# The order of the last loads on SyncE's queue, and a pool of their own for the last modulation products

## The chip, the cores and the metric

The kernel runs on one core of one Trainium2 chip. The metric is the time of one execution on the device in microseconds (us), of which the kernel before has three runs; beside them stands one execution recorded by the hardware profiler. The engines are named as in the profile: PE (TensorE matmuls; PEld is its weight load), DVE (VectorE), ACT (ScalarE), POOL (GpSimd) and SP (SyncE). SP computes nothing here: its queue (SPq) issues nearly all DMA transfers, one after the other.

## The reference

The kernel computes the output and all gradients of one adaLN-conditioned block. With x of shape 1x2048x512 (S = 2048 rows, D = 512 columns), F = 1792, and six modulation rows of 512 from `silu(c) @ w_mod`:

```python
mod = (_silu(c) @ w_mod).reshape(c.shape[0], 6, 1, -1)
sa, ca, ga, sb, cb, gb = (...)
h = _layernorm(x) * (1 + ca) + sa
x = x + ga * irfft2(rfft2(h) * (A_w_r + 1j * A_w_i))
h = _layernorm(x) * (1 + cb) + sb
r = relu(h @ w1 + b1)
x = x + gb * ((r * r) @ w2 + b2)
_out, _vjp = jax.vjp(_f, A_x, A_w_r, A_w_i, B_w1, B_b1, B_w2, B_b2, c, w_mod)
_grads = _vjp(grad_out)
```

Ten arrays come out: the block's output, and the gradients of x, of the two spectral filters, of w1, b1, w2, b2, c and w_mod. All are bfloat16.

## The kernel before

The 2048 rows lie as 16 row tiles of 128 rows (`NT = 16`), handled in pairs t = 0, 2, ..., 14. The 1792 hidden columns are 14 blocks of 128 (`NFC = 14`), numbered 0 to 13 here. The Fourier transforms are matmuls with tables of sines. The kernel goes forward through the spectral part and the two-layer part, then back; the forward part and most of the backward one end about 325 us into the span. What follows, and what the change touches, is the last stage (lines 1399 to 1513), in which four kinds of work are interleaved:

- **The gradient of w2**, `grad_w2` (line 1378). For each hidden block, PE adds up 16 matmuls (L1386) with the transposed block `hns[fc]` as weights and the scaled output gradient `g_sb` as the moving side. ACT copies the sum to a `gw` tile (L1387), and SPq stores it (L1388). Blocks 10 and 13 are done in two halves of 256 columns. The order of the products is 0, 1, 3, 2, 4, 5, 6, 7, 8, 9, first half of 10, 11, 12, second half of 10, both halves of 13.
- **The loads of the blocks**, `load_hn` (line 1201). Block fc was written to `h_dram` earlier, and comes back as a transposing DMA of 512 KB (L1206). Blocks 4 to 13 go into a ring of six tiles, `hn` 0 to 5, in the pool `endp`: block 4 is tile hn_0s, block 9 is hn_5s, and blocks 10, 11, 12, 13 take over tiles hn_0s, hn_1s, hn_2s, hn_3s, so that each must wait until PE is done with block 4, 5, 6 or 7.
- **The last step of the gradient of x**, for each pair of row tiles: `row_pair` (line 1448) and `row_end` (line 1470). PE makes the inverse transform (L372, L382), ACT copies it out (L1456), and DVE and ACT go back through the first normalisation. This reads two tiles per pair that `load_rows3` (line 1275) brings in: the normalised rows `n1` (L1279; shown as n, n_0s or n_1s in the profile) and the gradient so far, `gxl` (L1280). They go round between three places: the pairs t = 4 and 10 use n and gxl, t = 0, 6 and 12 use n_0s and gxl_0s, and t = 2, 8 and 14 use n_1s and gxl_1s. So the load for t = 14 must wait until DVE and ACT have done with the rows of t = 8. With `q1 = gh1 * n1` (L1461) PE adds up column sums into `acc1` (L1443).
- **The last two products of the modulation gradient**, `gm.emit` (line 454) for j = 0 and 1. After the last column sums ACT copies half of `acc1` (L1494) and DVE adds the halves to `acc1_sb` (L1496). A matmul (L459) spreads the row over 128 partitions, ACT copies it to `gmbc` and scales it into `gwm` (L468), and DVE multiplies it with a quarter of a slice of w_mod each time (L471; its `gm_junk` result is thrown away, only the sum is kept). `gm.load` (line 449) brings the slices, `wmc`, in.

The last lines add up the gradient of c: DVE (L1506, L1508), a transposing matmul (L1510), a copy (L1512) and a store (L1513, tile gcr).

**Pools.** A `Slots` pool gets one stretch of each partition's memory and a tile per name and buffer number; when a pool is released, a later one may take its memory over. The first instruction of an engine that uses such a new pool then waits for all that still uses the old memory. Line 1431 makes the pool `endp` when the last product of the w1 gradient is done. In the kernel before it holds the ring of blocks, the `gw`, `gh1`, `q1` and `gs` tiles, and the tiles of the last two modulation products as well.

**The order of the instructions** is written out by hand: `ORDER` (line 477) has a string of numbers per engine. Each number is an instruction of that engine in the order in which the program's text makes them, and `set_order` (line 574) chains the instructions in the order of the string. No planner chooses anything. An engine's queue is in order, SPq's too: if one instruction there waits for a semaphore, all behind it wait. DMA transfers share eight completion semaphores in turn, so a transfer also waits for the landing of the eighth before it.

Of the kernel before, what the change touches and what calls it, by code (L numbers as in the profile page):

```python
# [11 lines left out]
FP32 = mybir.dt.float32  # L12
BF16 = mybir.dt.bfloat16
# [5 lines left out]
D = 512  # L19
# [250 lines left out]
def unfold(nc, pool, y, w, n, name):  # L270

    u = pool.tile([P, n, 2, 2, P], BF16, name=name, bufs=1)
    w2 = w.rearrange("p n (e c d) -> p n e c d", e=2, c=2)
    nc.vector.tensor_tensor(u[:, :, 0], w2[:, :, 0], w2[:, :, 1], op=ALU.add)
    nc.vector.tensor_tensor(u[:, :, 1], w2[:, :, 0], w2[:, :, 1], op=ALU.subtract)
    y4 = y.rearrange("p n (k d) -> p n k d", k=4)
    nc.vector.tensor_tensor(y4[:, :, 0:4:2, :], u[:, :, :, 0], u[:, :, :, 1], op=ALU.add)
    nc.vector.tensor_tensor(y4[:, :, 3:0:-2, ::-1], u[:, :, :, 0], u[:, :, :, 1], op=ALU.subtract)
# [88 lines left out]
def spec_g2(tc, K, CS, t, tpool, pool, ahead=0):  # L367

    nc = tc.nc
    ps = pool.tile([P, D], FP32, name="psT")  # L370
    for i in range(4):
        nc.tensor.matmul(ps[:, P * i:P * i + P], lhsT=CS[:, t, i].rearrange("p a b -> p (a b)"), rhs=K["Cf"][:, i, :], start=True, stop=True)  # L372
    Tsb = tpool.tile([P, D], BF16, name="Tsb", bufs=4 if ahead else 2)
    K["Tsb"] = nc.scalar.activation(Tsb, ps, AF.Copy, scale=EF_S).ins
    return Tsb


def spec_g3(tc, K, Tsb, pool):

    nc = tc.nc  # L380
    psY = pool.tile([P, D], FP32, name="psY")
    nc.tensor.matmul(psY, lhsT=K["TAT"], rhs=Tsb, start=True, stop=True)  # L382
    return psY
# [57 lines left out]
class GMod:  # L441
# [12 lines left out]
    def emit(self, jc, q, row, pool, ppool, nbuf=2, last=False):  # L454
# [110 lines left out]
        "137 143 149 158 146 150 112 132 164 83 145 144 165 161 166 160 162 168 159 163 169 171 154 167 170 173 172 175 147 174 "  # L565
        "178 186 176 188 209 185 190 193 177 191 210 183 195 204 223 192 187 194 189 207-208 180 215 200 197 196 202 206 217 205 "
        "216 211 181 179 199 203 213 225 218 201 220 198 219 212 182 184 214 224 222 221 229 236 227 237 228 226 233 232 231 230 "
        "241 234 247 235 246 253 267-268 239 251-252 260 245 243 255 240 242 272 244 249 274 264 256 258 257 269 262 276 259 250 "
        "254 263 271 275 238 261 279 277-278 270 265-266 248 283 282 284 280 285 287 281 286 288 273 289"
    ),  # L570
}
# [22 lines left out]
def kernel(  # L594
# [602 lines left out]
    gm = GMod(tc, K, scf, gsc, wm_view, out9_view)  # L1197
    hnp = Slots(tc, name="hnp", bufs=1, side="right")
    hns, endp = [], {}
# [67 lines left out]
    def run_later(n=1):  # L1267
        if later:
            later[0][0] -= n
            if later[0][0] <= 0:  # L1270
                later.pop(0)[1]()
# [3 lines left out]
    def load_rows3(t):  # L1275
        if t < NT:
            pool, n = (endp["fp"], 1) if t % 6 == 4 else (fin, 2)
            rows3[t] = [pool.tile([P, 2, D], BF16, name=x, bufs=n) for x in ("n1", "gxl")]
            nc.sync.dma_start(rows3[t][0], n1_dram[t // 2])  # L1279
            K["rows"] = nc.sync.dma_start(rows3[t][1], gx1_dram[t // 2]).ins  # L1280
# [22 lines left out]
    def fill_w1(n):  # L1303
        for _ in range(n):
            if units:
                units.pop(0)()
# [110 lines left out]
    psX = Slots(tc, name="psX", bufs=1, space=PSUM)  # L1417
# [6 lines left out]
    def fill(n):  # L1424
        for _ in range(n):
            if units:
                fill_w1(1)
                if not units:
                    gwa.release()
                    gap.release()  # L1430
                    endp["hn"] = endp["gm"] = Slots(tc, name="endp", bufs=2)
            elif units2:
                units2.pop(0)()
                run_later()

    with Slots(tc, name="psE", bufs=2, space=PSUM) as psE, Slots(tc, name="psS1", bufs=1, space=PSUM) as psS1:

        acc1 = psS1.tile([P, D], FP32, name="acc1")
        late = Delayed(2)

        def colsums1(t, gh1, q1):
            for q, row in ((0, gh1[:, 0, :]), (32, q1[:, 0, :]), (64, gh1[:, 1, :]), (96, q1[:, 1, :])):
                nc.tensor.matmul(acc1[q:q + 32, :], lhsT=K["ones_q"], rhs=row, start=(t == 0), stop=(t == NT - 2), tile_position=(0, q))  # L1443

        def g2_pair(t):
            return [spec_g2(tc, K, CS, t + i, fp, psE, 60) for i in range(2)] if t < NT else None

        def row_pair(t, Ts):
            n1, gxl = rows3[t]
            gh1, q1 = [(endp["gm"].tile([P, 2, D], BF16, name=x, bufs=3) if "gm" in endp and t >= 6 else fp.tile([P, 2, D], BF16, name=x, bufs=2)) for x in ("gh1", "q1")]  # L1450
            gn = fp.tile([P, 2, D], BF16, name="gn")
            gs = (endp["gm"].tile([P, 2, D], BF16, name="gs", bufs=6) if "gm" in endp and t >= 6 else fp.tile([P, 2, D], BF16, name="gs", bufs=3))
            rr = fp.tile([P, 2, 4], FP32, name="rr")
            for i in range(2):
                psY = spec_g3(tc, K, Ts[i], psE)
                nc.scalar.copy(out=gs[:, i, :], in_=psY)  # L1456
            unfold(nc, fp, gh1, gs, 2, "unf_u")
            nc.vector.tensor_tensor(gn, gh1, modb[:, CA1_B, None, :].broadcast_to([P, 2, D]), op=ALU.mult)
            for i in range(2):
                nc.scalar.activation(gs[:, i, :], gn[:, i, :], AF.Copy, scale=inv1[:, t + i:t + i + 1], accum_out=rr[:, i, 0:1])  # L1460
            nc.vector.tensor_tensor(q1, gh1, n1, op=ALU.mult)  # L1461
            late.add(lambda: colsums1(t, gh1, q1))
            for i in range(2):
                jk = fp.tile([P, D], BF16, name="jk1", bufs=1)
                nc.vector.scalar_tensor_tensor(out=jk, in0=gs[:, i, :], scalar=K["onef"], in1=n1[:, i, :], op0=ALU.mult, op1=ALU.mult,
                                               accum_out=rr[:, i, 1:2])
            nc.vector.tensor_scalar(rr[:, :, 2:4], rr[:, :, 0:2], -1.0 / D, None, op0=ALU.mult)
            return t, n1, gxl, gn, gs, rr

        def row_end(t, n1, gxl, gn, gs, rr):  # L1470
            for i in range(2):
                nc.scalar.activation(gn[:, i, :], n1[:, i, :], AF.Identity, scale=rr[:, i, 3:4], bias=rr[:, i, 2:3])
            nc.vector.tensor_tensor(gs, gn, gs, op=ALU.add)
            gx = gs
            nc.vector.tensor_tensor(gx, gs, gxl, op=ALU.add)
            nc.sync.dma_start(out1_view[:, t:t + 2, :], gx)
            load_rows3(t + 6)

        Ts = g2_pair(0)
        for t in range(0, NT, 2):  # L1480
            fill(1)
            pair = row_pair(t, Ts)
            Ts = g2_pair(t + 2)
            if t < NT - 2:
                row_end(*pair)
            fill(1 if t % 4 == 0 and t < 12 else 0)
            if t == 10:
                grad_b2()
                gm.load(0, endp["gm"])
                gm.load(1, endp["gm"])  # L1490
        fill(3)
        late.flush()
        acc1_odd = endp["gm"].tile([64, D], FP32, name="acc1_odd", bufs=1)
        K["Tsb"] = nc.scalar.copy(out=acc1_odd, in_=acc1[64:128, :]).ins  # L1494
        acc1_sb = endp["gm"].tile([64, D], BF16, name="acc1_sb", bufs=1)
        nc.vector.tensor_tensor(acc1_sb, acc1[0:64, :], acc1_odd, op=ALU.add)  # L1496
        row_end(*pair)
        fill(1)
        for j in range(2):
            gm.emit(j, 32 * j, acc1_sb[32 * j:32 * j + 1, :], endp["gm"], psX, 4, True)  # L1500
            fill(1)
        while units2:
            fill(1)

        gst = fp.tile([P, 4], FP32, name="gst")
        nc.vector.tensor_reduce(gst, gsc.rearrange("p j d -> p d j"), axis=mybir.AxisListType.X, op=ALU.add)  # L1506
        gcb = fp.tile([P, 4], BF16, name="gcb")
        nc.vector.scalar_tensor_tensor(out=gcb, in0=t1, scalar=-1.0, in1=gst, op0=ALU.mult, op1=ALU.mult)  # L1508
        pg = psX.tile([4, P], BF16, name="mm")
        nc.tensor.transpose(pg, gcb, K["ident"])  # L1510
        gcr = fp.tile([4, P], BF16, name="gcr", bufs=1)
        nc.vector.tensor_copy(gcr, pg)  # L1512
        nc.sync.dma_start(out_8.rearrange("b (dc p) -> (b dc) p", p=P), gcr)  # L1513
# [8 lines left out]
    cdp.release()  # L1522
    cfp.release()
    utcs.release()
    endp["gm"].release()
    set_order(tc)

# [32 lines left out]
```

## Time and profile before

| | |
|---|---|
| median of 3 runs | 406.19 us (405.02 to 406.92) |
| the profiled execution | 405.56 us |
| its span, first to last instruction | 403.8 us |
| granted TensorE clock, mean | 0.991 |
| PE busy | 385.1 us (95%) |
| DVE busy | 341.9 us (85%) |
| ACT busy | 278.3 us (69%) |
| packets of the busiest DMA queue, share of 16 engines' span | 90.0% |

Busy time is the union of an engine's instructions; a pipelined matmul counts until its modelled end. The waits name, for each idle spot of an engine, the line that ran after it and what ended it. A row of a timeline gives start and duration in us, the engine, the line, and what is written from what. A DMA row of SPq is the issue alone, from the moment when its waits are over until the queue is free again; the transfer lands later. The trace's semaphore updates give the time of each landing (the completion marks).

### The profile page before, as it was taken

The numbers are of one execution on the slowest core, as the hardware profiler recorded it, in microseconds if no ns is written. First come the engines' busy times: TensorE is split into PE (matmuls) and PEld (weight loads), VectorE is DVE, ScalarE is ACT, GpSimd is POOL, SyncE is SP. The second block draws the span as 40 slices with busy tenths as digits, with TensorE's granted clock in tenths as the row PEclk, the third lists the DMA queues.
The fourth block names the chain that finished last, engine by engine and source line by source line (L and its number), as shares of the span: only waits on it lengthen the run. The fifth ranks groups of instructions, "written<-read, shape, count | busy, mean of one in ns | idle before, by whom it ended". The sixth has DMA issues, their size and how long they took to land.

```text
span 403.8 us, 6936 instructions
## 1 busy us (share of the span) xinstructions
PE 385.1 (95%) x2403; PEld 201.8 (50%) x2428; DVE 341.9 (85%) x831; ACT 278.3 (69%) x501; POOL 14.0 (3%) x56
## 2 busy tenths in 40 slices
PE   4899999999999999999999999899999999899887
PEld 1345566765444444444444444455655665444345
DVE  5989978969896899989898999938789967697795
ACT  4569899889870695279536857358667546898595
POOL 4520100000000000000000000000000000000000
PEclk9699999999999999999999999999999999999999
DMA  8999999587595899779977889969999999999997
GB/s 251 239 210 280 238 205 273 157 193 262 160 217 111 215 217 199 178 171 235 206 208 160 201 206 237 272 187 302 279 274 271 256 326 161 192 259 236 232 270 262
DMA packets 141643, 90.97 MB, mean 225 GB/s; under 512 B 95778, under 2 KB 127528, under 8 KB 141096
## 3 DMA queue, kind: packets, MB, share of 16 engines
q1 hardware_dynamic: 140900, 89.93, 90.0%
q10 hardware_dynamic: 708, 0.59, 0.5%
q8 instruction: 19, 0.31, 0.3%
q14 instruction: 16, 0.13, 0.1%
HBM read 36.35 MB, written 33.19 MB: 172 GB/s over the span
## 4 chain that ended last, share of the span: by engine, by line
PE 64%; DVE 12%; ACT 8%; SPq 7%; DMA 6%; issue 2%; DVEq 0%; ACTq 0%
PE og_0s L1042 8%; PE og_1s L1042 8%; PE mm_0s L1287 6%; PE mm_1s L1287 5%; PE mm_1s L1386 4%; PE mm_1s L841 4%; PE mm_1s L1013 4%; PE mm_0s L1386 3%; PE mm_0s L841 3%; PE mm_0s L1013 3%; DMA w2T<-in_B_w_dram 3%; PE pst L1013 2%; SPq L1206 2%; SPq L693 2%; ACT AE L336 2%
## 5 line engine op out<-in xcount | busy, mean ns | idle before, releaser
L1287 PEld LDWEIGHTS <-h_sb 128*128 128x128 bf16 x256 | 24.7, 98 | 21.4 <-issue 0.4
L1042 PEld LDWEIGHTS <-gab 128*128 128x128 bf16 x224 | 21.5, 98 | 25.1 <-DVE gab L1020 0.6
L1013 PEld LDWEIGHTS <-w 128*128 128x128 bf16 x224 | 21.3, 98 | 25.0 <-issue 1.7
L841 PEld LDWEIGHTS <-w2T 128*128 128x128 bf16 x224 | 21.2, 98 | 22.3 <-issue 2.9
L1287 PE MATMUL mm_0s<-gab,h_sb 128*128 128x384 bf16 (+1 forms) x160 | 30.2, 342 | 0.0
L1042 PE MATMUL og_0s<-w1T,gab 128*128 128x512 bf16 x110 | 25.7, 379 | 0.4 <-DVE gab L1020 0.3
L1042 PE MATMUL og_1s<-w1T,gab 128*128 128x512 bf16 x108 | 25.3, 379 | 0.2
L336 ACT ACTIVATE AE<-psB 128x1024 bf16<-128x1024 f32 x16 | 22.2, 1387 | 2.6 <-PE psB L332 2.6
L1013 PE MATMUL mm_1s<-h2T,w 128*128 128x512 bf16 x84 | 21.6, 379 | 0.0
L1287 PE MATMUL mm_1s<-gab,h_sb 128*128 128x512 bf16 (+1 forms) x96 | 20.8, 370 | 0.0
L1013 PE MATMUL mm_0s<-h2T,w 128*128 128x512 bf16 x80 | 20.5, 379 | 0.0
L841 PE MATMUL mm_1s<-gT_0s,w2T 128*128 128x512 bf16 x56 | 15.4, 394 | 0.9 <-DMA w2T<-in_B_w_dram 0.8
L841 PE MATMUL mm_0s<-gT_0s,w2T 128*128 128x512 bf16 x56 | 15.3, 397 | 0.8 <-DMA w2T<-in_B_w_dram 0.5
L372 PEld LDWEIGHTS <-utcs 128*128 128x128 bf16 x128 | 10.3, 97 | 10.4 <-issue 4.1
L1013 PE MATMUL pst<-h2T,w 128*128 128x512 bf16 x60 | 15.4, 379 | 0.0
L841 PE MATMUL mm_1s<-gT_1s,w2T 128*128 128x512 bf16 x56 | 14.4, 379 | 0.1
L841 PE MATMUL mm_0s<-gT_1s,w2T 128*128 128x512 bf16 x56 | 14.4, 379 | 0.1
L1386 PE MATMUL mm_0s<-g_sb,hn_1s 128*128 128x512 bf16 x62 | 14.2, 379 | 0.1
L845 ACT CAST gab<-mm_1s 128x512 bf16<-128x512 f32 x20 | 12.4, 621 | 2.3 <-PE mm_1s L841 2.3
L1386 PE MATMUL mm_1s<-g_sb,hn_0s 128*128 128x512 bf16 (+1 forms) x63 | 12.7, 352 | 0.1
L332 PEld LDWEIGHTS <-utcs 128*128 128x128 bf16 x128 | 9.3, 98 | 4.9 <-issue 1.8
L407 ACT ACTIVATE inv<-l_mv_1s,eps 128x2 f32<-128x2 f32 x4 | 1.2, 304 | 15.0 <-DVE l_mv_1s L952 15.0
(652 smaller groups left out, 1054.2 us busy)
## 6 DMA issues: line engine op xcount, KB each, us to landing
w<-in_B_w_dram SPq DMA_DIRECT2D x2, 1792.0 KB, 9.0
Z<-wz_dram SPq DMA_DIRECT2D x4, 514.0 KB, 4.4
Xb<-xs_dram SPq DMA_DIRECT2D x4, 514.0 KB, 6.1
x_sb<-in_A_x_dram SPq DMA_DIRECT2D x2, 1024.0 KB, 6.6
n_dram<-x_sb SPq DMA_DIRECT2D x4, 512.0 KB, 4.8
h_dram<-h2r SPq DMA_DIRECT2D x8, 256.0 KB, 2.3
h_sb<-h_dram SPq DMA_DIRECT2D x4, 512.0 KB
g_sb<-in_grad_out_dram SPq DMA_DIRECT2D x2, 1024.0 KB
```

The source lines that it names most:

```text
L332: nc.tensor.matmul(ps[:, hh, P * co:P * co + P], lhsT=UT[:, c, 2 * gi + hh, :, :], rhs=K["Cd"][:, P * c:P * c + P], start=not extra, stop= ...
L336: nc.scalar.activation(dst, ps.rearrange("p r (s e f) -> p (r s) e f", s=2, e=2), AF.Copy, scale=EF_S)
L372: nc.tensor.matmul(ps[:, P * i:P * i + P], lhsT=CS[:, t, i].rearrange("p a b -> p (a b)"), rhs=K["Cf"][:, i, :], start=True, stop=True)
L407: nc.scalar.activation(dst, var, AF.Sqrt, bias=K["eps"])
L693: q.dma_start(gT[b].rearrange("p j c q -> p (j c) q"), g_view[:, TB * b:TB * b + TB, :].rearrange("p j d -> p (j d)"), transpose=True)
L841: nc.tensor.matmul(ps, lhsT=w2T[:, dc, fc * P:(fc + 1) * P], rhs=gT[b][:, :, dc, :], start=(dc == 0), stop=(dc == 3))
L845: nc.scalar.copy(out=gaT[b][:, fc, :], in_=ps)
L1013: nc.tensor.matmul(ps, lhsT=w1[:, dc, (fc + i) * P:(fc + i + 1) * P], rhs=h2T[b][:, :, dc, :], start=(dc == 0), stop=(dc == 3))
L1042: nc.tensor.matmul(ps, lhsT=lhs(fc), rhs=rhs[:, fc, :], start=(fc == 0), stop=(fc == NFC - 1))
L1206: nc.sync.dma_start(hns[fc], h_dram[fc, :, :], transpose=True)
L1287: nc.tensor.matmul(blocks(ps, fb), lhsT=h2_sb[:, t, dc * P:(dc + 1) * P], rhs=gh_rows(t, fb), start=(t == 0), stop=(t == NT - 1))
L1386: nc.tensor.matmul(ps[:, 0:w], lhsT=hns[fc][:, t, :], rhs=g_sb[:, t, c:c + w], start=(t == 0), stop=(t == NT - 1))
```

## The change

Two edits. The first moves seven numbers of SPq's string in `ORDER`: 256, 258, 259, 262, 272, 274 and 276, which are transfers of the last stage, stand in other places. In the program this reads as follows, with the issues from the load of block 9 or 10 to that of block 12:

| place | before | after |
|---|---|---|
| 1 | block 10 (hn_0s) | block 9 (hn_5s) |
| 2 | gxl_1s, t = 8 | gxl_1s, t = 8 |
| 3 | n, t = 10 | n, t = 10 |
| 4 | block 11 (hn_1s) | n_0s, t = 12 |
| 5 | store of gw_4s | store of gw_4s |
| 6 | block 9 (hn_5s) | block 10 (hn_0s) |
| 7 | n_0s, t = 12 | n_1s, t = 14 |
| 8 | store of gs_0s, t = 6 | store of gs_0s, t = 6 |
| 9 | store of gw_6s | store of gw_6s |
| 10 | n_1s, t = 14 | block 11 (hn_1s) |
| 11 | block 12 (hn_2s) | gxl_0s, t = 12 |
| 12 | gxl_0s, t = 12 | block 12 (hn_2s) |

The strings of the other engines, and all else of SPq's, are as before. The second edit makes a pool `endq` beside `endp`, and puts the tiles wmc, gmbc, gm_junk, gwm, acc1_odd and acc1_sb of the last two modulation products into it.

```diff
@@ ORDER["SP"]
-        "241 234 247 235 246 253 267-268 239 251-252 260 245 243 255 240 242 272 244 249 274 264 256 258 257 269 262 276 259 250 "
+        "241 234 247 235 246 253 267-268 239 251-252 260 245 243 255 240 242 256 244 249 258 264 272 262 257 269 274 259 276 250 "
@@ fill
                     gap.release()
                     endp["hn"] = endp["gm"] = Slots(tc, name="endp", bufs=2)
+                    endp["q"] = Slots(tc, name="endq", bufs=2)
@@ the loop over the row tiles, and what follows it
             if t == 10:
                 grad_b2()
-                gm.load(0, endp["gm"])
-                gm.load(1, endp["gm"])
+                gm.load(0, endp["q"])
+                gm.load(1, endp["q"])
         fill(3)
         late.flush()
-        acc1_odd = endp["gm"].tile([64, D], FP32, name="acc1_odd", bufs=1)
+        acc1_odd = endp["q"].tile([64, D], FP32, name="acc1_odd", bufs=1)
         K["Tsb"] = nc.scalar.copy(out=acc1_odd, in_=acc1[64:128, :]).ins
-        acc1_sb = endp["gm"].tile([64, D], BF16, name="acc1_sb", bufs=1)
+        acc1_sb = endp["q"].tile([64, D], BF16, name="acc1_sb", bufs=1)
...
-            gm.emit(j, 32 * j, acc1_sb[32 * j:32 * j + 1, :], endp["gm"], psX, 4, True)
+            gm.emit(j, 32 * j, acc1_sb[32 * j:32 * j + 1, :], endp["q"], psX, 4, True)
@@ the end
     utcs.release()
+    endp["q"].release()
     endp["gm"].release()
```

## The prediction

> **What bounds the kernel now.** I read the page first, then the waits and the engines' timelines from 325 us on, since the change touches nothing before that.
>
> ```profile
> PE 385.1 (95%) x2403; PEld 201.8 (50%) x2428; DVE 341.9 (85%) x831; ACT 278.3 (69%) x501; POOL 14.0 (3%) x56
> DMA  8999999587595899779977889969999999999997
> ```
>
> TensorE (PE) has work 95% of the span, and its matmuls of one product follow each other every 0.216 us (3.45 us for 16), so only its few idle spots can be won. The DMA engines stay at nine tenths through the last quarter. The waits after 325 us name the idle spots, in us in total, times, longest:
>
> ```profile
> ACT gw_0s L1387 <- DMA out_dram<-gw_1s: 2.2, 1, 2.2
> DVE q_0s L1461 <- DMA n_0s<-n_dram: 1.5, 1, 1.5
> PE mm L459 <- DVE acc_sb L1496: 1.1, 1, 1.1
> DVE jk L1465 <- DMA n<-n_dram: 1.1, 1, 1.1
> PE mm_0s L1386 <- DMA hn_5s<-h_dram: 0.8, 1, 0.8
> PE acc L1443 <- DVE q_1s L1461: 0.7, 1, 0.7
> ```
>
> PE waits for block 9 (hn_5s), for the column sums of the last rows (q_1s, t=14), and for their total (acc_sb). The last two hang on VectorE (DVE), which itself waits for rows t=10 (n), t=12 (n_0s) and t=14 (n_1s). SyncE's queue (SPq), in the order of its issues (start, duration), shows why they are late:
>
> ```profile
> 366.04 4.00 SPq L1206 DMA_TRANSPOSE hn_0s<-h_dram  x1
> ...
> 370.76 0.37 SPq L1279 DMA_DIRECT2D n<-n_dram  x1
> 371.23 2.62 SPq L1206 DMA_TRANSPOSE hn_1s<-h_dram  x1
> ...
> 374.53 2.21 SPq L1206 DMA_TRANSPOSE hn_5s<-h_dram  x1
> 376.85 0.52 SPq L1279 DMA_DIRECT2D n_0s<-n_dram  x1
> ...
> 378.42 0.43 SPq L1279 DMA_DIRECT2D n_1s<-n_dram  x1
> 378.94 4.19 SPq L1206 DMA_TRANSPOSE hn_2s<-h_dram  x1
> ...
> 387.33 3.70 SPq L1206 DMA_TRANSPOSE hn_3s<-h_dram  x1
> ...
> 401.14 0.28 SPq L1513 DMA_DIRECT2D out_dram<-gcr  x1
> ```
>
> Blocks 10 (hn_0s) and 11 (hn_1s) stand ahead of block 9, and PE uses them much later:
>
> ```profile
> 378.99 3.63 PE L1386 MATMUL mm_0s<-g_sb,hn_5s 128*128 128x512 bf16 x15 [0.83 <-DMA hn_5s<-h_dram]
> ...
> 384.60 1.92 PE L1386 MATMUL mm_1s<-g_sb,hn_0s 128*128 128x256 bf16 x16
> ...
> 387.97 3.63 PE L1386 MATMUL mm_0s<-g_sb,hn_1s 128*128 128x512 bf16 x15
> ...
> 391.85 3.63 PE L1386 MATMUL mm_1s<-g_sb,hn_2s 128*128 128x512 bf16 x16
> ```
>
> One more reading is needed. A transposing load holds SPq for 2.0 to 5.1 us, not 0.5, and its issue ends about when the transfer ahead of it lands; its completion marks follow 2.0 to 3.0 us after the issue's end. So the queue is a line in which each transfer waits for the one before, and its order decides what lands when.
>
> **The change, part by part.**
>
> *Order of the queue.* Between 366 and 384 us the queue carries four block loads and seven others. [...] Nothing is added or removed; gxl_0s moves ahead of block 12. No other engine's order changes. Landings now, from the completion marks: block 9 378.9, n(t=10) 373.9, n(t=12) 380.4, n(t=14) 383.2. Estimated landings after: block 9 takes the place of block 10, which landed at 372.2. gxl_1s came 1.1 after that, n(t=10) another 0.6: 373.9, as now. n(t=12) comes 0.7 to 1.4 later, 374.6 to 375.3. Block 10 follows at about 377.2, n(t=14) 1.1 to 1.7 behind it, 378.3 to 378.9; block 11 at 381.4, block 12 at 384.5.
>
> *What each is worth.* Block 9: 0.83 us of PE idle go. What is late next is q_1s, so this alone gives nothing at the end. Rows: from DVE's start on n(t=10) at 373.99 to q_1s at 383.32 are 9.33 us, of which DVE sat idle 1.54 for n(t=12) and 0.31 for n(t=14). Without these it reaches q(t=12) at 378.9 (row there 3.6 us before) and q_1s at 381.5 (2.6 us before). So q_1s, the total and the product at L459 come 1.85 us sooner; I take 1.8, since the waits' hand-over of about 0.05 stays. From L459 (387.66) on PE is without a gap, so the shift holds to its last product. If the rows' cover is gone, each us of lateness past 378.9 and 381.5 comes back one for one.
>
> *Blocks moved back.* Block 10 lands 5.6 us ahead of its use (384.60 - 1.8 = 382.8), block 11 4.8 us (386.2), block 12 5.5 us (390.0). Free; the price beyond that cover is again one for one.
>
> *Waits on the queue.* The n(t=14) load overwrites the rows of t=8 and must wait for ScalarE's (ACT) second L1472 on them, which ended at 375.56. Its place used to come at 378.4; now it comes at about 375.1. Cost 0 to 0.5, I take 0.2. Behind it wait gs_0s, gw_6s and blocks 11 and 12, all with more cover. The n(t=12) load waits for t=6 rows, done by 366.5; blocks 10, 11, 12 for PE's use of blocks 4, 5, 6, done by 362.7, 365.9 and 370.8: nothing.
>
> *Pool.* In their own pool the wmc, gmbc, junk, gwm and acc1 tiles take other addresses, and what is left of the endp pool no longer lies over the memory of Xb and the w1 gradients. ACT's first gw copy then waits for no store: the 2.20 us before 343.96 go, and with them PE's small gaps from 345.58 to 352.21 (0.45 + 0.26 + 0.75 + 0.20 = 1.66). That is not added to the 1.8: DVE still cannot pass n(t=10) at 373.9, so it only waits there longer. In exchange wmc's loads and acc1's tiles wait for stores that landed by 343.9, while they run at 353 and 386: nothing.
>
> *The queue's own end.* After block 13's issue ends at 391.03, SPq issues 17 stores up to 401.42 with 8.7 us of issue time and ordinary steps between them; I count 0.5 us of real waits there (0.33 before gs_3s). The last store, gcr, was ready at 401.11, and the queue free at 401.05. So the queue is as late as the engines, and the end can come sooner only by 0.5 plus what block 13's issue gains. That gain: by the steps above block 12's issue ends at 382.3 instead of 383.13, and gxl_0s (0.7) is already done: 1.5. But the row for n(t=14) shows a hold of 1.74 after the store ahead of it where 0.4 to 0.7 is usual, and it can come again elsewhere: 0.1. In the middle 0.8. Sum: 0.5 + 0.8 = 1.3 us sooner, bounds 0.6 and 1.8 (then DVE's path binds).
>
> *Rule against row.* The Trainium skill (DMA: Bandwidth & Descriptors, "Issuing engines are not separate DMA queues") says that the sequencer's time to start a DMA is usually small against the DMA. By that the queue binds nothing and the sum is the full 1.8. The rows (2.0 to 5.1 us of issue for blocks that land 2 to 3 us later) say otherwise; I take 1.3.
>
> Sum: profiled run 405.56 with span 403.8 becomes 404.3 with span 402.5. The three runs' median, 406.19, lies 0.6 above that run; the same shift gives **404.9**.
>
> **Rivals.** (1) *Full shift, and more:* the queue flows without the 1.4 us holds, n(t=10) too lands earlier, and the gain reaches 2.1 to 2.7. For it: two long holds in this stretch (1.74, and 2.08 for the store of gs_1s) that need not recur. Against: the same amount of data, and the last 17 stores. 403.8. (2) *Nothing moves:* the transfers take the same total whatever their order, block 13's issue stays at 391.0, and SPq's last stores give back all but 0.5: 405.7. For it: the nine tenths of DMA; against: the idle bits between marks. (3) *Slower:* the holds become more. Place: blocks 10 to 12, which now stand behind a row load, a store and a gxl load. Price: every us by which block 12's issue ends after 383.1 shifts block 13 and the 17 stores one for one. With a hold of 1.5 at each of the three blocks, 4.5 in all against the 1.5 gained by the order, block 13's issue ends 3.0 us later: 406.19 + 3.0 - 0.5 = 408.7. The end is later than now from 0.5 us of delay on, and measurably from 2.5. For it: issues up to 5.0 us (block 6); against: blocks behind one another took 2.0 (block 7).
>
> **Numbers.** 0.5% is 2.0 us; the three runs spread over 1.9, so less can hardly be told from no change. Likeliest, 1.3 sooner: 0.38 (own range 404.2 to 405.6). Rival 1: 0.33; rival 2: 0.13; rival 3: 0.16, a quarter of it under 2 us. Faster by over 0.5%: rival 1, and 0.07 of the likeliest's lower edge, which the median of another few runs can put past 2.0: 0.40. Slower: three quarters of rival 3, and 0.03 for what I can't name: 0.15. Within: 0.45. Range 403.0 to 407.2: it takes in rival 2, two thirds of rival 1 and the mild part of rival 3.
>
> **What would show it.** Right: block 9's product without an idle spot in front of it; no DVE wait at L1461 for n_0s and n_1s; the wait at "jk" for n(t=10) grown from 1.1 to 2 us or more; ACT's 2.2 us at L1387 gone; block 13's issue ending near 390.2; SPq back to back to its last store. Wrong: n(t=14)'s issue held beyond 376; PE waiting for hn_0s, hn_1s or hn_2s; block 13's issue after 391; or the last stores ready late because DVE's chain from 374 on grew.

## The result and the profile after

Twenty runs of each kernel: 406.36 us (404.77 to 408.10) before, 404.68 us (402.88 to 406.74) after. The ratio is 0.9958, 95% interval 0.9944 to 0.9973, so the change saves 1.7 us (1.1 to 2.3). The forecast was 1.3 us, and 404.9. The profiled execution after took 404.68 with a span of 402.9, against 405.56 and 403.8 before: this pair is 0.9 apart, because the execution profiled before lay 0.8 under the median of its kernel and the one after on it. So the two profiles show the places, and the medians the size.

From the new line at 1432 on, each line of the kernel has moved down by one (L1443 is now L1444, L1461 is L1462). The page's first and DMA rows, after:

```profile
PE 384.2 (95%) x2403; PEld 202.0 (50%) x2428; DVE 341.9 (85%) x831; ACT 278.5 (69%) x501; POOL 14.1 (3%) x56
...
DMA  8989999478495798778977889969999899999997
```

Nothing here tells the kernels apart. The waits after 325 us do:

```profile
PE mm_0s L1386 <- DMA hn_1s<-h_dram: 1.6, 1, 1.6
...
DVE jk L1466 <- DMA n<-n_dram: 1.3, 1, 1.3
...
PE mm L459 <- DVE acc_sb L1497: 0.8, 1, 0.8
...
DVE q_1s L1462 <- DMA n_1s<-n_dram: 0.7, 1, 0.7
```

Gone are ACT's 2.2 at L1387, DVE's 1.5 for n_0s, and PE's waits for block 9 (0.8) and for q_1s (0.7 at the place of t = 14). The wait for n_1s in the last line is that of t = 8, at 365.43. New is PE's wait of 1.6 for block 3 (tile hn_1s at 348), which no step of the prediction had. SPq's issues, after:

```profile
366.41 3.63 SPq L1206 DMA_TRANSPOSE hn_5s<-h_dram  x1
...
370.78 0.37 SPq L1279 DMA_DIRECT2D n<-n_dram  x1
371.25 0.36 SPq L1279 DMA_DIRECT2D n_0s<-n_dram  x1
...
372.18 3.12 SPq L1206 DMA_TRANSPOSE hn_0s<-h_dram  x1
375.42 0.51 SPq L1279 DMA_DIRECT2D n_1s<-n_dram  x1
...
376.97 2.37 SPq L1206 DMA_TRANSPOSE hn_1s<-h_dram  x1
...
380.30 3.09 SPq L1206 DMA_TRANSPOSE hn_2s<-h_dram  x1
...
387.01 3.34 SPq L1206 DMA_TRANSPOSE hn_3s<-h_dram  x1
...
400.07 0.30 SPq L1514 DMA_DIRECT2D out_dram<-gcr  x1
```

By the completion marks the rows landed at 374.0 (t = 10, as before), 375.1 (t = 12, 5.3 sooner) and 378.5 (t = 14, 4.7 sooner). PE's products from block 9 on, where no idle time is noted there was none:

```profile
377.82 3.62 PE L1386 MATMUL mm_0s<-g_sb,hn_5s 128*128 128x512 bf16 x15
...
383.00 1.91 PE L1386 MATMUL mm_1s<-g_sb,hn_0s 128*128 128x256 bf16 x16 [0.28 <-ACT gw_0s L1387]
385.75 0.38 PE L459 MATMUL mm<-acc_sb,ones_sq 1*128 1x512 bf16 x1 [0.84 <-DVE acc_sb L1497]
```

The first product at L459, before:

```profile
387.66 0.39 PE L459 MATMUL mm<-acc_sb,ones_sq 1*128 1x512 bf16 x1 [1.13 <-DVE acc_sb L1496]
```

It comes at 385.75 instead of 387.66, 1.91 sooner. The end did not follow all the way. DVE, at the row of t = 10, at q_1s and at the very last copy:

```profile
374.08 0.75 DVE L1466 SCALAR_TENSOR_TENSOR jk<-gs_2s,onef,n 128x512 bf16<-128x512 bf16 x1 [1.33 <-DMA n<-n_dram]
...
381.39 0.68 DVE L1462 TENSOR_TENSOR q_1s<-gh_1s,n_1s 128x1024 bf16<-128x1024 bf16 x1
...
399.00 0.21 DVE L1513 COPY gcr<-mm 4x128 bf16<-4x128 bf16 x1 [1.79 <-PE mm L1511]
```

The same two, q_1s and the last copy, before:

```profile
383.32 0.69 DVE L1461 TENSOR_TENSOR q_1s<-gh_1s,n_1s 128x1024 bf16<-128x1024 bf16 x1 [0.31 <-DMA n_1s<-n_dram]
...
400.90 0.21 DVE L1512 COPY gcr<-mm 4x128 bf16<-4x128 bf16 x1 [1.75 <-PE mm L1510]
```

gcr is ready at 399.21 (401.11 before), but SPq issues its store at 400.07: it stood 0.86 in the queue, where before it stood none. It is not gcr alone that is late: the store ahead of it, that of block 8 (gw_0s), landed at 401.76, only 0.08 before gcr. The line of stores as a whole ends there. The completion marks say the same of the two ends. Before, ACT's own last store, at the end of PE's chain, landed last (402.80; SPq's last 402.61). After, SPq's lands last (401.84), and ACT's at 401.39. PE's chain gained 1.4, the queue 0.8, the later of the two 1.0.

### The profile page after: what moved, and what is told of

It is laid out like the page before. It is cut to its first block, busy times and chain, and to the rows that moved or that the text cites. A ratio compares the mean times of both kernels' runs of the same rounds, so it can differ in the third digit from the quotient of the medians.

```text
span 402.9 us, 6928 instructions
## 1 busy us (share of the span) xinstructions
PE 384.2 (95%) x2403; PEld 202.0 (50%) x2428; DVE 341.9 (85%) x831; ACT 278.5 (69%) x501; POOL 14.1 (3%) x56
## 5 line engine op out<-in xcount | busy, mean ns | idle before, releaser
L1386 PEld LDWEIGHTS <-hn_0s 128*128 128x128 bf16 x80 | 7.7, 98 | 6.4 <-issue 0.7
```

Source lines behind the costliest of these rows:

```text
L1386: nc.tensor.matmul(ps[:, 0:w], lhsT=hns[fc][:, t, :], rhs=g_sb[:, t, c:c + w], start=(t == 0), stop=(t == NT - 1))
```

## The experiments

Three chips, one for each group of four, and in each group the kernel before was run beside: its median was 405.36, 408.83 and 404.94 us. So only kernels of one group are compared in microseconds.

| kernel | median us | ratio to before | 95% interval |
|---|---|---|---|
| order_only | 404.85 | 0.9985 | 0.9963 to 1.0006 |
| pool_only | 405.61 | 1.0005 | 0.9987 to 1.0024 |
| block9_first | 405.27 | 0.9995 | 0.9979 to 1.0012 |
| rows_first | 404.83 | 0.9984 | 0.9969 to 0.9998 |
| after_again | 405.99 | 0.9936 | 0.9908 to 0.9965 |
| tail_act | 406.04 | 0.9947 | 0.9926 to 0.9969 |
| row10_early | 408.37 | 0.9987 | 0.9960 to 1.0015 |
| row10_early_tail_act | 407.50 | 0.9967 | 0.9937 to 0.9996 |
| after_third | 404.35 | 0.9965 | 0.9936 to 0.9995 |
| order_again | 404.89 | 0.9989 | 0.9964 to 1.0015 |
| plain_blocks | 402.51 | 0.9920 | 0.9890 to 0.9950 |
| stores_act | 403.22 | 0.9952 | 0.9925 to 0.9979 |

Differences between two kernels of a group are those of the means of their 10 to 12 runs, with the middle 95% of what resampling these runs gives.

**The two edits apart.** order_only is the changed kernel without the pool endq:

```diff
-                    endp["q"] = Slots(tc, name="endq", bufs=2)
-                gm.load(0, endp["q"])
-                gm.load(1, endp["q"])
+                gm.load(0, endp["gm"])
+                gm.load(1, endp["gm"])
...
```

> Only SyncE's new order; the tiles of the last two products stay in the pool endp. Theory (the rows for t = 12 and 14 land sooner, VectorE's two waits for them go, and the end is shared with SyncE's queue): all of the changed kernel's 1.7 us, so 404.5 to 405.0 beside 406.4 before, with ScalarE's wait of 2.2 us at L1387 still there. Rival (the pool gives the gain, by ScalarE's 2.2 us and TensorE's gaps of 1.66 us): 406.2 to 406.6, nothing.

pool_only keeps endq and has SP's old string:

```diff
-        "... 240 242 256 244 249 258 264 272 262 257 269 274 259 276 250 "
+        "... 240 242 272 244 249 274 264 256 258 257 269 262 276 259 250 "
```

> Only the pool endq; SyncE's order as before the change. Theory: the work up to 352 us runs earlier, but VectorE then waits longer for the rows of t = 10, which land at 373.9 as before: 406.1 to 406.6, no change. Rival: about 1 to 1.7 us sooner, 404.7 to 405.4.

The pool alone gave nothing, as the theory had it, and its profile shows where the lead of the earlier stretch went. Its waits after 325 us:

```profile
PE mm_0s L1386 <- DMA hn_5s<-h_dram: 2.1, 1, 2.1
...
DVE jk L1466 <- DMA n<-n_dram: 1.8, 1, 1.8
...
DVE q_0s L1462 <- DMA n_0s<-n_dram: 1.4, 1, 1.4
```

ACT's wait at L1387 is gone, and PE begins block 8 at 373.40 instead of 374.54. Then PE waits 2.1 for block 9 (0.8 before) and DVE 1.8 for the row of t = 10 (1.1 before); L459 stands at 387.79, as before.

The order alone came out 0.5 us faster by the medians, with an interval that holds none and 1.5; the theory wanted all of the change's gain. Beside the pool alone it is 0.7 faster (0.0 to 1.4). Its profile has the whole of PE's gain (no wait for n_0s, for n_1s of t = 14 or for block 9; L459 at 385.99, 1.67 sooner than before; ACT's wait still there, at 1.0). Most of it is lost again at the queue's end:

```profile
399.24 0.21 DVE L1512 COPY gcr<-mm 4x128 bf16<-4x128 bf16 x1 [1.76 <-PE mm L1510]
```

```profile
400.54 0.30 SPq L1513 DMA_DIRECT2D out_dram<-gcr  x1
```

gcr is ready at 399.45 and stands 1.09 us in the queue; the last transfer lands at 402.35, only 0.45 sooner than the last one before. That left it open whether the pool gives part of the gain once the order is changed, or whether two chips differ. So the two were run once more, on one chip.

> The changed kernel, beside the order alone on one chip. Theory (the pool is absorbed by the wait for the rows of t = 10): the two have the same time within 0.3 us. Rival (order and pool add up): the changed kernel 0.5 to 1.1 sooner than the order alone, as the comparisons on two different chips would have it (1.7 and 0.6 us).

> SyncE's new order alone, again. Theory: as the changed kernel, within 0.3 us. Rival: 0.5 to 1.1 later than the changed kernel.

The changed kernel is 0.5 us faster than the order alone (from 1.1 faster to 0.3 slower). That does not tell the theory (at most 0.3 apart) from the rival (0.5 to 1.1). In three comparisons the changed kernel's ratios are 0.9958, 0.9936 and 0.9965 (the last is 0.9985 by the medians; one of its twelve runs, 407.56, lies 2.6 above the next), in two the order's are 0.9985 and 0.9989. This leans to a share of the pool, some tenths of a us up to one. No profile shows a place for it: in the three profiles of the changed kernel and in that of tail_act (below) DVE waits 0.8 to 1.8 us for the row of t = 10, which should swallow any lead; and at the queue's end gcr stood 0.83 to 1.80 us in the changed kernel's three, 1.09 and 1.50 in the two of the order alone. It stays open.

**Which transfer matters.** block9_first has only the blocks in the order of their use, the rows where they were:

```diff
-        "... 240 242 272 244 249 274 264 256 258 257 269 262 276 259 250 "
+        "... 240 242 256 244 249 272 264 274 258 257 269 262 276 259 250 "
```

> The kernel before, with only the blocks in the order of their use on SyncE's queue (9, 10, 11, 12, each at a place where a block stood); the rows stay where they were. Theory: TensorE's 0.83 us ahead of block 9 go, VectorE's waits for the rows of t = 12 and 14 (1.5 and 0.3 us) stay, q_1s is as late as before: 406.1 to 406.6. Rival (block 9 sets the end): 0.8 sooner, 405.4 to 405.7.

It came out as the theory said, no change (0.9995). From its waits after 325 us:

```profile
DVE q_0s L1461 <- DMA n_0s<-n_dram: 1.6, 1, 1.6
PE acc L1443 <- DVE q_1s L1461: 1.4, 1, 1.4
```

PE's 0.83 for block 9 is gone, and its wait for q_1s has grown from 0.70 to 1.43, by 0.73. DVE's wait of 0.3 for the row of t = 14 did not stay, but q_1s starts at 383.32, as before. L459 stands at 387.65 (387.66 before). A wait that is taken away ahead of a later one is only moved.

rows_first is the opposite: the rows forward, block 9 behind block 10:

```diff
-        "... 240 242 256 244 249 258 264 272 262 257 269 274 259 276 250 "
+        "... 240 242 272 244 249 258 264 256 262 257 269 274 259 276 250 "
```

> The changed kernel's order without its pool, but with blocks 9 and 10 exchanged, so that block 9 comes only after the rows of t = 12 and lands at an estimated 377.8, where TensorE wants it at about 378. Theory: the rows are the gain; 0.0 to 0.4 us of wait for block 9 is hidden behind q_1s, so as the order alone, 404.5 to 405.1. Rival (block 9 has to come first): TensorE's wait of 0.8 us or more stays and shows at the end, 405.4 or more.

404.83 us beside 404.85 of order_only, 0.1 apart (0.6 faster to 0.5 slower). Block 9 landed at 377.2, and PE took it at once:

```profile
377.53 3.62 PE L1386 MATMUL mm_0s<-g_sb,hn_5s 128*128 128x512 bf16 x16
```

So it is the rows that are worth something (the interval of this run, 0.9969 to 0.9998, just leaves out no change); block 9 need only be there by 377.5, and it was, behind block 10.

**Which end binds.** These three are built on the changed kernel, which was run again beside them.

> The changed kernel once more, so that the next three and the runs of the single edits stand beside it on one chip and one set of runs of the kernel before. By the first comparison 1.7 us sooner than before (1.1 to 2.3); by the steps of the prediction 1.3; if the order alone (0.5 to 0.6 sooner) is all of the change, about 0.6.

tail_act takes two of SPq's last stores to ACT's queue; the numbers behind them in SP's and ACT's strings follow:

```diff
-            (nc.scalar if c > 0 and fc == NFC - 1 else nc.sync).dma_start(...)
+            (nc.scalar if fc in (8, NFC - 1) else nc.sync).dma_start(...)
```

> The changed kernel, with two stores that SyncE issues third and second to last (first half of block 13, block 8) moved to ScalarE's queue, into the 1.4 us in which ScalarE waits for the last product; the last store (gcr) stays. Theory (SyncE's queue sets the end): SyncE's last issue ends 0.9 to 1.0 us sooner, gcr is issued as soon as it is ready (399.2), the last landing becomes that of ScalarE's own last store, 0.45 sooner than now: 0.4 to 0.5 sooner than the changed kernel. Rival (TensorE's chain alone sets the end): the same time as the changed kernel, within 0.1.

row10_early moves the load of the rows of t = 10 (number 249) two places forward in SP's order, directly ahead of block 9 (256), with gxl_1s (244) behind both:

```diff
-        "... 240 242 256 244 249 258 ..."
+        "... 240 242 249 256 244 258 ..."
```

> The changed kernel, with the load of the rows of t = 10 one transfer later block 9, that is ahead of block 9, gxl_1s behind it. Theory (SyncE's queue sets the end): VectorE's wait of 1.3 us for these rows goes, L459 and TensorE's last product come about 1.1 us sooner, but SyncE's last store does not: 0 to 0.3 sooner than the changed kernel. Rival (TensorE's chain sets the end): 0.9 to 1.2 sooner.

> Both edits together. Theory (two chains end nearly together, so that only both edits show): SyncE's end 1.0 and TensorE's 1.1 us sooner, 0.9 to 1.1 sooner than the changed kernel, more than the sum of the two alone. Rival (no chain but TensorE's counts): as with the rows alone, 0.9 to 1.2; told apart by the two single runs.

row10_early is 2.0 us slower than the changed kernel (1.1 to 2.9), which neither theory had. Its row of t = 10 comes in time, and DVE does not wait for it. The last copy and SPq's queue in its profile:

```profile
399.58 0.21 DVE L1513 COPY gcr<-mm 4x128 bf16<-4x128 bf16 x1 [2.09 <-PE mm L1511]
```

```profile
367.46 0.37 SPq L1279 DMA_DIRECT2D n<-n_dram  x1
367.88 4.31 SPq L1206 DMA_TRANSPOSE hn_5s<-h_dram  x1
...
389.14 4.41 SPq L1206 DMA_TRANSPOSE hn_3s<-h_dram  x1
...
402.47 0.31 SPq L1514 DMA_DIRECT2D out_dram<-gcr  x1
```

gcr is ready at 399.79, and its store leaves 2.7 us later. Counted from the issue of gxl_0s for t = 6, which stands ahead of all transfers that moved, gcr is ready after 33.43 us (33.85 to 34.26 in the three profiles of the changed kernel), and SPq's last issue ends after 36.42 (35.01 to 36.02). So PE's chain is shorter here and the queue's longer, and the time went with the queue. The profiles show only about half of the 2.0: the execution profiled here (407.03) lies 1.3 under its kernel's median, that of the changed kernel on this chip (407.50) 1.5 above.

The sum of the five transposing holds (a hold is the duration of an issue; blocks 9 to 13), and the time from the issue of gxl_0s for t = 6 to the end of block 13's issue and to the end of the second store of gs_2s, six stores later, in the profiles, us:

| kernel | five holds | gxl_0s to block 13 | gxl_0s to gs_2s |
|---|---|---|---|
| before | 16.72 | 26.08 | 30.28 |
| changed (three profiles) | 15.55 to 15.77 | 24.99 to 25.66 | 28.86 to 29.52 |
| order alone (two) | 15.84, 15.85 | 25.63, 26.16 | 29.38, 30.06 |
| rows_first | 15.97 | 25.48 | 29.49 |
| tail_act | 16.12 | 25.32 | 29.12 |
| row10_early, with tail_act | 17.97, 18.03 | 27.19, 27.25 | 30.03, 30.11 |
| stores_act | 16.61 | 24.41 | 28.12 |

In both profiles with the row ahead block 9's hold is 4.31 and 4.66 (3.63 to 4.05 without it), as a line of transfers would have it; but block 10's is no shorter for it, and block 13's is 4.41 and 4.37 instead of the 3.27 to 3.65 of the changed kernel, the order alone and tail_act. This microsecond at block 13 is not lost. In the other kernels one of the stores behind block 13 is held 1.2 to 1.6 us, in these two none is, and from block 13's issue to the end of gs_2s they take 7.25 and 7.23 us, the changed kernel 6.93 to 7.21. What the early row costs the queue is read from the last column: 0.5 to 1.3 us. As elsewhere (see below), block 13's hold ended when the transfer ahead of it landed; that store, gs_1s, landed 4.9 us after its issue's end in both, 3.6 to 3.7 in the changed kernel. Why it did is open.

With tail_act on top 0.8 us come back (1.8 faster to 0.2 slower), near the 1.0 that two issues cost; both edits together are 1.2 slower than the changed kernel (0.3 to 2.2), where 0.9 to 1.1 sooner was expected. On the changed kernel itself tail_act brought nothing: 406.04 beside 405.99, 0.0 apart (0.8 faster to 0.8 slower), where 0.4 to 0.5 was expected. In its profile gcr is ready at 401.17 and issued at 401.20, so the queue no longer held it; but DVE waited 1.8 us for the row of t = 10 there, and PE's chain ended last. An effect of 0.4 is within the spread of these runs.

**What makes the queue a line.** The hold of a transposing load ends with the transfer that SPq issued ahead of it: in the fourteen profiles, from 338 us on, 137 of 144 such issues ended between 0.6 us before and 0.15 after the landing of that transfer. plain_blocks loads blocks 9 to 13 without the transposition:

```diff
-            nc.sync.dma_start(hns[fc], h_dram[fc, :, :], transpose=True)
+            nc.sync.dma_start(hns[fc], h_dram[fc, :, :].rearrange("p (t c) -> p t c", c=P)) if fc >= 9 else nc.sync.dma_start(hns[fc], h_dram[fc, :, :], transpose=True)
```

> The changed kernel, but blocks 9 to 13 are loaded without the transposition (same bytes, same tiles), so that the last five blocks of the gradient of w2 are not the reference's. Theory (the transposing loads make SyncE's queue a line): five issues of 0.5 us instead of 2.4 to 3.6, the rows of t = 10 land before VectorE wants them, TensorE's chain comes 1.1 us sooner and SyncE's last store no longer binds: 1.2 to 1.9 sooner than the changed kernel. Rival (the bytes bind, the DMA engines are busy anyway): less than 0.5 sooner.

1.9 us faster than the changed kernel (1.0 to 2.9), at the upper end of what the theory gave. SPq's issues there:

```profile
363.75 0.42 SPq L1206 DMA_DIRECT2D hn_5s<-h_dram  x1
...
381.97 0.34 SPq L1206 DMA_DIRECT2D hn_3s<-h_dram  x1
...
395.91 0.28 SPq L1514 DMA_DIRECT2D out_dram<-gcr  x1
```

The five issues take 1.99 us instead of 15.77 (the changed kernel on this chip), for the same 512 KB each, and gcr (ready at 395.88) is issued 0.03 later. From issue to landing such a block takes 5.1 to 6.5 us here, and 5.2 to 7.0 in the first profile of the changed kernel, about the same; but here the next transfers are issued meanwhile. The bytes are not free of charge either: DVE still waits 0.40 for the row of t = 10. From 367 to 382 us the DMA engines' mean busy share is 0.86, 0.61 and 0.96 in stretches of 5 us, where the changed kernel on this chip has 1.09, 0.95 and 1.05 (above 1 the times of packets overlap). That is no clean comparison: the stretches do not hold the same work, the queue here stood from 367.46 to 373.02 until ACT was done with the rows of t = 8, and the two profiled executions are the fastest of their ten (400.27) and the slowest of their twelve (407.56). So the run shows what the transposition of the five loads costs, 1.9 us, not how much of it is the queue and how much the engines.

stores_act leaves the work whole and takes three stores from between the block loads to ACT's queue:

```diff
-            (nc.scalar if c > 0 and fc == NFC - 1 else nc.sync).dma_start(...)
+            (nc.scalar if c > 0 and fc == NFC - 1 or fc in (4, 6) else nc.sync).dma_start(...)
...
-            nc.sync.dma_start(out1_view[:, t:t + 2, :], gx)
+            (nc.scalar if t == 6 else nc.sync).dma_start(out1_view[:, t:t + 2, :], gx)
```

> The changed kernel, with three stores (gw of block 4, rows of t = 6, gw of block 6) that stand between the block loads on SyncE's queue moved to ScalarE's queue, behind its copy at 375.76, where ScalarE waits 2.4 us. Theory (SyncE's issues bind, not the transfers): SyncE's end comes 1.3 us sooner (three issues of 0.42), TensorE's chain then sets the end: 0.4 to 0.5 sooner than the changed kernel. Rival (the DMA engines are full, whichever queue issues): the holds of the block loads grow by what the issues gain, the time stays within 0.2 of the changed kernel.

It has the lowest median of the kernels that compute everything: 403.22 us, 1.0 faster than the changed kernel on its chip (0.3 to 1.8) and 0.48% faster than the one before. The block loads in its profile:

```profile
365.35 3.69 SPq L1206 DMA_TRANSPOSE hn_5s<-h_dram  x1
...
370.71 3.73 SPq L1206 DMA_TRANSPOSE hn_0s<-h_dram  x1
...
375.15 3.75 SPq L1206 DMA_TRANSPOSE hn_1s<-h_dram  x1
```

```profile
398.35 0.28 SPq L1514 DMA_DIRECT2D out_dram<-gcr  x1
```

Both sides were partly right. The holds grow, by 0.84 in sum against the changed kernel of the same chip (15.77), as the rival said; but the stretch from gxl_0s to block 13 shrinks by 1.25 (25.66 to 24.41; by 0.6 and 1.2 against the other two profiles of the changed kernel), about what three issues cost. gcr is ready at 398.32 and issued at 398.35, where it stood 0.83 to 1.80 us in the three profiles of the changed kernel. From DVE's start on the row of t = 10 to L459 are 11.64 us, as in the changed kernel (11.67), so what was gained lies behind that: at the queue's end.

## Why the prediction was right, point by point

The mechanism, rows that come sooner and then the queue's end as the limit, is what the profiles show. That the number came so near owes something to luck, at two places below.

- **Block 9, nothing by itself.** Right, and shown: the wait of 0.83 turns up as 0.73 more at q_1s in block9_first.
- **The rows.** Right to 0.1: q_1s at 381.39 (381.5 forecast), L459 1.91 sooner (1.8). Landings of 375.1 and 378.5 (374.6 to 375.3 and 378.3 to 378.9 forecast). pool_only and block9_first, without the rows' new places, gain nothing; rows_first has what the order has. But the sum puts the whole 1.3 on the order, and the two runs of the order alone have 0.6 and 0.4, with intervals that hold both none and 1.3.
- **Covers of the blocks moved back.** Enough, with less to spare. Block 10 landed at 377.8, block 11 at 382.8, block 12 at 385.5 (377.2, 381.4 and 384.5 forecast), against uses at 383.0, 386.07 and 389.95. The estimate spaced the blocks 4.2 and 3.1 us apart; the marks say 4.9 and 2.8. The completion marks of the blocks do not always follow the issue's end by 2.0 to 3.0 us: block 11's came 3.4 after it, block 13's 3.6, and block 5's 4.4 in the profile before.
- **The wait in front of the load for t = 14.** Under 0.1 in this profile, 0.2 taken. It is real: in after_again this load was held 0.9 us, until ACT's L1473 on the rows of t = 8 was done (378.78; issued at 378.80). A size that changes from run to run.
- **The pool.** That DVE only waits longer for n(t = 10) is right for the pool alone. That this wait grows to 2 us or more is not: it is 1.33, and 0.83 to 1.83 in the other five profiles that have the pool, the transposing loads and this row in its place. The step that failed is the one that let PE's 1.66 us of small gaps go without naming what PE would meet next: block 3, for which it waited 1.64 in the profile after, and 0.8 to 2.4 in five of the other eight with the pool. That the pool's share with the new order is nothing, as the sum has it, was not shown; if it has one, the order's term was too large by as much, and the sum right in part by luck.
- **The queue's end.** That it binds holds in the profile, and the two terms came out a little under the forecast: block 13's issue ends at 390.34 (390.2 forecast), 0.69 sooner (0.8 taken), and the 17 stores take 10.04 us instead of 10.39, back to back, 0.35 shorter (0.5 taken). 0.69 + 0.35 = 1.04, which is what SPq's end gained. The steps inside the 0.69 are not those of the prediction. Block 12's issue ends at 383.39, 0.26 later than before, where 382.3 was forecast; from there to block 13's issue are 3.62 us instead of 4.20, 0.58 less (0.7 for gxl_0s); and block 13's own hold is 0.36 shorter (3.34 instead of 3.70), which no step had. That the middle of 0.1 and 1.5 fitted was in part luck.
- **Rule against row.** The medians' 1.7 (1.1 to 2.3) lies nearer to the 1.8 of the rule than to the 1.3 of the row, and its interval holds both, so the time alone does not decide. The rows and runs speak for the row: 15.55 us of holds for five issues, gcr 0.86 us late at the queue, 1.9 us gained where the holds go, 1.0 where three issues leave the queue, and 2.0 lost in row10_early, where PE's chain is shorter and the queue longer.
- **Rivals.** "Nothing moves" is out. The full shift (403.8) is not out by the time, since the interval reaches 2.3; but its mechanism did not happen in the profile, where the row of t = 10 landed as before (374.0) and the queue held the end. The slower rival did not happen to the changed kernel, with blocks 10 to 12 held 2.4 to 3.1 us. row10_early is a case of its kind, a longer queue that makes a slower kernel, though not one for one with the holds.

## What to carry to other kernels

Where one queue issues nearly all transfers, its last store is an end of its own beside the compute engines' chain: read when the last result is ready and when its store is issued, and cost a reordering on both. A long hold of one issue is not by itself a loss: see whether one further down the queue is shorter for it. Of several late transfers, move the one whose consumer waits last; an earlier one only lengthens the next wait. A store that an idle engine can issue instead may be worth its issue time even where the DMA engines are busy: it was for three stores between the transposing loads (stores_act), and was not seen for two at the very end (tail_act).

## What was not expected of the hardware

- The same 512 KB held the issuing queue 2.4 to 3.6 us with the transposition (the changed kernel's first profile) and 0.34 to 0.45 without it, though from issue to landing it took 5 to 7 us either way. With it, the hold ended about when the transfer ahead landed.
- One 256 KB load placed directly ahead of a transposing load, instead of two places behind it, made the kernel 2.0 us slower (1.1 to 2.9). In the profiles the five transposing holds are 2.2 us longer in sum (15.7 to 18.0, both on one chip), of which one microsecond, at block 13, comes back at a store behind it.
- The pair of transposing loads ahead of 348 us, whose place the change leaves as it was, held the queue between 6.95 and 9.61 us in fourteen profiles, and the kernel before ran at 404.9 to 408.8 us by the median on four occasions: more from one occasion to the next than the change is worth.
